# Moving the weight sums of the first up block and of the second gate/up block behind the first gate group's products

## The chip, the cores and the metric

The kernel runs on one core of one Trainium2 chip. The metric is the device time of one execution in microseconds (us); less is better. All times below are of this kernel on such a core. In the profile PE is the matmul engine (TensorE), PEld its weight loads, DVE the vector engine, ACT the scalar engine, POOL GpSimd, and SP the engine that issues most of the DMAs.

## The reference

```python
x  = A_x                                   # 2048 tokens x 1024
xn = layernorm(x)
q, k, v = split_heads(xn @ wqkv)           # 32 heads of 32
o  = phi(q) (phi(k)^T v) / (phi(q) . sum phi(k))
s  = o @ wo                                # the attention branch
g  = silu(xn @ w_gate)                     # 1024 x 3584
u  = xn @ w_up                             # 1024 x 3584
y  = (g * u) @ w_down                      # 3584 x 1024
out = x + s * silu(y)
```

All inputs are bf16. `phi(t)` is `t + 1` for positive `t` and `exp(t)` otherwise, plus 1e-6.

## The kernel before

The work has three stages, and PE goes through them in one order that is written out by hand. The first normalises and transposes the tokens and makes q, k, v and the sums over the tokens; the second makes the attention output and its projection with `wo` (`s_sb`, stored to `s_dram`); the third is the gated network: gate and up products, `h = silu(gate) * up` stored to `h_dram`, and from about 570 us the product with `w_down`.

**Seven products for eight.** Most matrix products are done by blocks of 2 x 2 with seven block products instead of eight, on sums of blocks. In the gate/up stage one *group* is one block of 256 columns of `w_gate` or `w_up` (index `m`, 14 of them; `gu` is 0 for gate and 1 for up) against 1024 tokens (`p`, 2 of them). Each of the seven products (M3, M4, M1, M5, M2, N7, N6) is a set of four matmuls of 128 x 128 by 512, recorded on line 131. M3 and M4 use the weights as loaded (`wg_sb`, `wu_sb`). The other five use sums of weight blocks, which four DVE operations (lines 152 to 155, `wsum_ops`) write to `ws_all`; `sum_w(m, gu)` (line 166) issues these four. `ws_all` has two slots for `m`, used in turn, and two for `gu`.

**A group's steps** (class `Group`, line 994):
- `part_a`: M3 into the accumulator X, then ACT copies X to `n` (line 1007); M4 into Y, then DVE makes `q = n + Y` (line 1011).
- `part_b`: M1 into Z, then DVE makes `u = Z + q` (line 1017); M5 is added onto X, and X goes to the sink on ACT; M2 is added onto Y, and Y goes to the sink on ACT.
- `part_c`: N7 onto X and N6 onto Y, each followed by a DVE subtraction from `u` (line 1026), into `cg` for gate and `up` for up.

X, Y and Z are banks of the accumulator memory, eight in all, taken in turn. The order on PE is: part_a of a group, part_c of the group before it, part_b of the group. So a group's first four sets (its own M3 and M4, the older group's N7 and N6) need no weight sums of its own; M1 is the first that does.

**What sets the order.** In the second stage the order on PE, DVE, ACT, POOL and SP is that of the source (`FRONT_ORDER` and SP, line 921). In the third stage only PE's and POOL's is (`PE_ORDER`, line 987); DVE, ACT and SP get theirs from a scheduler that places an operation once its inputs are there by its own reckoning. Operations of the third stage can be placed by it between those of the second. Each engine then works through its own list in order.

**Around the change.** The end of the second stage projects the last tokens in two groups of the same seven products, `sg` and `sh`, each ending in two DVE subtractions to `s_sb` (line 908), each stored by a DMA that ACT issues (line 884). Between them stand the first two calls of `sum_w`:

```python
            sg.part_c()
            sum_w(0, 0)
            sh.part_b()
            sh.part_c()
            sum_w(0, 1)
```

In the loop of the third stage (line 1186) `sum_w(m + 1, gu)` is issued behind each group's `part_b` when `p` is 0 (line 1220).

`gate(insts, after)` (line 80) adds, for each instruction given, an edge from `after`; with its default it is marked as one without synchronisation, for the scheduler only. `marks["mm"]` is the matmul issued last by `products` (line 131).

Of the kernel before, what the change touches and what calls it, by code (L numbers as in the profile page):

```python
# [21 lines left out]
def kernel(  # L22
# [57 lines left out]
    def gate(insts, after, sync=False):  # L80
        if after is None:
            return
        for d in insts:
            tc.add_manual_dep(d.ins, after.ins.name, SYNCD if sync else SCHED, reason="prefetch gate")

    marks = {}
# [61 lines left out]
    def wsum_ops(w, ws):  # L148

        ws = ws.rearrange("p (k c) -> p k c", k=HD)  # L150
        tt = nc.vector.tensor_tensor
        return [lambda: tt(out=ws[:, :, 0:P], in0=w[:, 0:HD, 0:P], in1=w[:, HD:DC, P:2 * P], op=ALU.add),
                lambda: tt(out=ws[:, :, P:3 * P], in0=w[:, 0:HD, :], in1=w[:, HD:DC, :], op=ALU.add),
                lambda: tt(out=ws[:, :, 3 * P:4 * P], in0=w[:, HD:DC, P:2 * P], in1=w[:, HD:DC, 0:P], op=ALU.subtract),
                lambda: tt(out=ws[:, :, 4 * P:5 * P], in0=w[:, 0:HD, 0:P], in1=w[:, 0:HD, P:2 * P], op=ALU.subtract)]
# [7 lines left out]
    wraw = {}  # L163
    wsum = {}

    def sum_w(m, gu):
        wsum[(m, gu)] = ws_all[:, m % 2, gu]
        for op in wsum_ops(wraw[(m, gu)], wsum[(m, gu)]):
            op()

    def w_operands(m, gu):
        return block_operands(wraw[(m, gu)], wsum[(m, gu)])

    def load_w(m, after=None, sync=False):
        cols = slice(m * FW, (m + 1) * FW)
        wg_sb = wgu.tile([P, DC, FW], BF16, name="wg_sb", tag="wg_sb")
        d1 = nc.sync.dma_start(out=wg_sb[:], in_=wg_v[:, :, cols])
        wu_sb = wgu.tile([P, DC, FW], BF16, name="wu_sb", tag="wu_sb")
        d2 = nc.sync.dma_start(out=wu_sb[:], in_=wu_v[:, :, cols])
        gate([d1, d2], after, sync=sync)  # L180
        wraw[(m, 0)] = wg_sb
        wraw[(m, 1)] = wu_sb
# [573 lines left out]
    with ExitStack() as p2:  # L756
# [12 lines left out]
        def emit_KVZ():  # L769
            for j in range(NJ):  # L770
                g0 = j * GPT
                ng = min(GPT, G - g0)
                nc.vector.tensor_tensor(out=KVZ[:, g0:g0 + ng, 0:P], in0=kvz_ps[j][:, 0:ng, 0:P],
                                        in1=mask[:, None, :].to_broadcast([P, ng, P]), op=ALU.mult)
                nc.vector.tensor_tensor(out=KVZ[:, g0:g0 + ng, P:P + HPG],
                                        in0=kvz_ps[j][:, 0:ng, P:P + 1].to_broadcast([P, ng, HPG]),
                                        in1=sel[:, None, :].to_broadcast([P, ng, HPG]), op=ALU.mult)
# [33 lines left out]
        def emit_OT():  # L811
            while o_ready:
                b, t, o_sb = o_ready.popleft()
                r0 = b * TB + t * P
                nc.scalar.dma_start(out=o_dram[r0:r0 + P, :], in_=o_sb[:])
                nc.sync.dma_start_transpose(out=oT_of(b)[:, :, t * P:(t + 1) * P], in_=o_dram[r0:r0 + P, :])
                if (b, t) in load_at:
                    for m in load_at[(b, t)]:
                        load_w(m)
# [94 lines left out]
        def s_unit():  # L914
            emit_S(*units.popleft())

        def nd_tile():
            if nds:
                emit_ND(*nds.popleft())

        with tc.manual_schedule(engines=FRONT_ORDER | {ET.SP}):

            qb, qc = QGroup(NPASS - 1, NM_Q - 2), QGroup(NPASS - 1, NM_Q - 1)
            for c in range(NCC):
                nc.sync.dma_start(out=wo_sb[:, :, c * CW:(c + 1) * CW], in_=wo_v[:, :, c * CW:(c + 1) * CW])
            emit_KVZ()
            qa.part_b()
            nd_tile()
            qb.part_a()
            emit_OT()  # L930
            qa.part_c()
            nd_tile()
            qb.part_b()
            emit_OT()
            nd_tile()
            qb.part_c()
            emit_OT()


            rows = deque((grp, i) for grp in (qa, qb, qc) for i in range(2))  # L940
            nd_at = {1, 2, 4, 6, 8, 10, 11, 13, 15, 16, 17, 19, 20}
            row_at = {0, 1, 3, 5, 7, 9}
            wo_at = {10, 11, 12, 14, 18}
            sum_at = {23: lambda: groups[0].sums()}
            q_at = {0: qc.part_a, 2: qc.part_b, 3: qc.part_c}
            assert len(nd_at) == len(nds) and len(row_at) == len(rows)
            n7 = TPB * NCC
            groups = [SGroup(t) for t in range(0, TPB, 2)]
            for u in range(len(units) - n7):
                if u in q_at:  # L950
                    q_at[u]()
                if u in nd_at:
                    nd_tile()
                if u in row_at:
                    grp, i = rows.popleft()
                    grp.part_d(i)
                if u in wo_at:
                    out, a, b, op = wo_sums.popleft()
                    gate([nc.gpsimd.tensor_tensor(out=out, in0=a, in1=b, op=op)], marks["phi"], sync=True)
                if u in sum_at:  # L960
                    sum_at[u]()
                s_unit()
                emit_OT()
            sg, sh = groups
            sg.part_a()
            sh.sums()
            sg.part_b()
            sh.part_a()
            sg.part_c()
            sum_w(0, 0)  # L970
            sh.part_b()
            sh.part_c()
            sum_w(0, 1)
    p12.close()
    ps12.close()

# [109 lines left out]
    def slots_x(t):  # L1086
        return t[:].rearrange("p c (h t) -> p (c h) t", t=CW).bitcast(BF16)
# [4 lines left out]
    def slots_w(t):  # L1092
        return t[:].rearrange("p (a b) f -> p a (b f)", f=FW, b=CW // FW)

    def slots_wd(t):
        return t[:].rearrange("p k (a f) -> p (k a) f", f=CW)
# [87 lines left out]
    with tc.manual_schedule(engines=PE_ORDER):  # L1184
        prev = None
        for m, p in order:
            if p == 0 and m + PREF < NM:
                load_w(m + PREF)
            if (m, p) == (NM - 2, 0):
                sl5 = Slots()  # L1190
                for _ in range(2):
                    sl5.add(slots_w(wgu.tile([P, DC, FW], BF16, name="wg_sb", tag="wg_sb")), 4)
                    sl5.add(slots_w(wgu.tile([P, DC, FW], BF16, name="wu_sb", tag="wu_sb")), 4)
                sl1 = Slots()
                for _ in range(2):
                    sl1.add(slots_wd(wdst.tile([P, 2, D], BF16, name="wdr", tag="wdr")), 4)
                for _ in range(2):
                    sl1.add(wdst.tile([P, 3, CW], BF16, name="wdsA", tag="wdsA")[:], 3)
                    sl1.add(wdst.tile([P, 2, CW], BF16, name="wdsB", tag="wdsB")[:], 2)
                WD["M5"] = load_wd("M5", sl5.take(NM))  # L1200
            gs = GateSink()
            for gu in range(2):
                sink = gs if gu == 0 else UpSink(gs, m, p)
                grp = Group(w_operands(m, gu), x_operands(p), HD, sink)
                grp.part_a()
                if prev is not None:
                    prev.part_c()
                if gu == 0 and (m, p) == (NM - 2, NPASS - 1):
                    slx, sls = Slots().add(slots_x(xnT[0]), 16), Slots().add(slots_xs(XS[0]), 20)
                    load_h(0, (NM - 2,))  # L1210
                    WD["M3"] = load_wd("M3", slx.take(NM))
                    WD["M4"] = load_wd("M4", sls.take(NM))
                    sa5 = sls.take(4)
                    spare = Slots()
                    spare.free = sl1.free + sls.free + slx.free + sl5.free
                    WD["M1"] = load_wd("M1", spare.take(NM))
                grp.part_b()
                prev = grp
                if p == 0 and m + 1 < NM:
                    sum_w(m + 1, gu)  # L1220
                if gu == 0 and (m, p) in wd_at:
                    prep_wd(wd_at[(m, p)])
        hp0 = hps[0]
        h0_ops = {"M4": lambda k: hp0[:, 1, k, P:2 * P], "M3": lambda k: hp0[:, 0, k, 0:P]}
        first = Group(h0_ops, WD, NM, None)
        first.part_a()
        prev.part_c()
# [120 lines left out]
```

## Time and profile before

| | us |
|---|---|
| median of 3 runs | 748.28 |
| lowest and highest of them | 747.86, 748.52 |
| the profiled execution | 747.96 |
| its span, first to last instruction | 746.2 |
| granted share of PE's clock | 0.999 |

The span is what the profile covers; the profiled execution is 1.8 us longer than it. The busy time of each engine stands on the page that the prediction shows. A matmul is listed with a duration, but the next one starts before that has passed, so PE's time is best read from start to start. In the timeline each row has its start and its duration in us, the engine, the line, the operation, the tile written and the tiles read; the number in brackets is the time that the engine stood idle just before, and what ended it. In the waits view each row has who waited for whom, the total in us, how often, and the longest.

### The profile page before, as it was taken

Reading aid. Unit: us, or ns where it says so; the run is one execution under the profiler, and the core shown is the slowest. Engines: PE = TensorE matmul, PEld = TensorE weight load, DVE = VectorE, ACT = ScalarE, POOL = GpSimd, SP = SyncE. Lnnn points to the kernel's source line nnn. Section 1 sums busy time; section 2 is a strip of 40 time slices with the busy share of each in tenths; the row PEclk is TensorE's granted clock in tenths of the full one; section 3 lists DMA queues with packets and bytes.
Section 4 is the critical chain, followed back from the end, with each engine's and each line's share of the span. In section 5 each row is a group of like instructions: output and inputs, shape, how many; then the busy total and the mean of one; then the engine's idle time right before and its main releaser. Section 6 shows DMA issues by size and latency. Waiting matters only on the chain.

```text
span 746.2 us, 9886 instructions
## 1 busy us (share of the span) xinstructions
PE 736.9 (99%) x3661; PEld 347.0 (47%) x3700; DVE 517.4 (69%) x955; ACT 272.3 (36%) x476; POOL 69.9 (9%) x106
## 2 busy tenths in 40 slices
PE   9999999999999999999999999999999999999997
PEld 4544444455544444444444444444444444444454
DVE  6889896688768767787678867776655754445554
ACT  4444574755223343434343333434342111111111
POOL 3210000000730000000000000000000221121220
PEclk9999999999999999999999999999999999999999
DMA  9756000316689553655337643455779745554200
GB/s 313 260 161 170 1 0 1 113 44 156 198 230 278 149 149 101 188 174 158 109 97 204 184 127 105 150 161 156 265 255 344 284 171 183 184 184 170 98 29 29
DMA packets 132464, 118.09 MB, mean 158 GB/s; under 512 B 33728, under 2 KB 112704, under 8 KB 131136
## 3 DMA queue, kind: packets, MB, share of 16 engines
q1 hardware_dynamic: 127520, 108.68, 47.1%
q10 hardware_dynamic: 4896, 8.78, 3.5%
q8 instruction: 29, 0.48, 0.3%
q14 instruction: 19, 0.16, 0.1%
HBM read 70.52 MB, written 39.58 MB: 148 GB/s over the span
## 4 chain that ended last, share of the span: by engine, by line
PE 96%; DMA 2%; DVE 1%; issue 0%; ACT 0%; DVEq 0%; ACTq 0%
PE X L131 29%; PE Y L131 29%; PE Z L131 10%; PE kv_ps L455 9%; PE s_ps L829 5%; PE qX L131 3%; PE qY L131 3%; PE kY L131 2%; PE kX L131 2%; DMA wg_sb<-in_B_w_gate_dram 1%; PE nd_ps L790 1%; PE kvz L484 1%; PE qZ L131 1%; PE kZ L131 1%; DMA xp<-in_A_x_dram 0%
## 5 line engine op out<-in xcount | busy, mean ns | idle before, releaser
L131 PEld LDWEIGHTS <-ws_all 128*128 128x128 bf16 x1424 | 138.1, 98 | 164.0 <-issue 1.9
L1011 DVE TENSOR_TENSOR q<-n,Y 128x512 f32<-128x512 f32 x63 | 43.3, 688 | 104.4 <-PE Y L131 103.2
L131 PEld LDWEIGHTS <-xs 128*128 128x128 bf16 (+1 forms) x736 | 69.6, 98 | 76.5
L1281 POOL TENSOR_TENSOR o_out<-y,xres 128x512 bf16<-128x512 f32 x29 | 35.1, 1210 | 495.1 <-DVE y L1280 495.1
L131 PE MATMUL Y<-xs,ws_all 128*128 128x512 f16 (+3 forms) x308 | 70.3, 360 | 0.0
L131 PE MATMUL X<-xnT,ws_all 128*128 128x512 f16 (+1 forms) x278 | 70.1, 379 | 0.2
L131 PE MATMUL Y<-xnT,ws_all 128*128 128x512 f16 x224 | 57.5, 379 | 0.8 <-DVE q L1011 0.8
L131 PE MATMUL X<-xs,ws_all 128*128 128x512 f16 x224 | 57.5, 379 | 0.0
L131 PE MATMUL Z<-xs,ws_all 128*128 128x512 f16 x224 | 57.5, 379 | 0.0
L1135 ACT ACTIVATE g<-cg 128x512 bf16<-128x512 f32 x56 | 35.3, 630 | 54.4 <-DVE cg L1026 54.4
L1017 DVE TENSOR_TENSOR u<-Z,q 128x512 f32<-128x512 f32 x63 | 43.2, 686 | 15.9 <-PE Z L131 15.9
L1135 ACT ACTIVATE g<-X 128x512 bf16<-128x512 f32 x28 | 16.7, 597 | 99.0 <-PE X L131 99.0
L1007 ACT COPY n<-X 128x512 f32<-128x512 f32 x63 | 36.9, 585 | 30.8 <-PE X L131 27.6
L455 PEld LDWEIGHTS <-xnT 128*128 128x128 f16 x320 | 30.7, 98 | 36.0 <-DVE xnT L427 0.5
L1160 DVE TENSOR_TENSOR ho<-g,up 128x1024 bf16<-128x1024 bf16 x56 | 38.2, 685 | 0.5
L455 PE MATMUL kv_ps<-wk_sb,xnT 128*128 128x512 bf16 x156 | 36.9, 379 | 0.6 <-DVE xnT L427 0.3
L1280 DVE TENSOR_TENSOR y<-y,s_in 128x512 f32<-128x512 f32 x31 | 22.2, 717 | 21.4 <-ACT y L1274 15.8
L455 PE MATMUL kv_ps<-wv_sb,xnT 128*128 128x512 bf16 x155 | 35.9, 379 | 0.2
L131 PEld LDWEIGHTS <-wu_sb 128*128 128x128 bf16 x224 | 21.9, 98 | 26.4
L131 PEld LDWEIGHTS <-wg_sb 128*128 128x128 bf16 x224 | 21.9, 98 | 26.4
L1274 ACT ACTIVATE y<-X 128x512 f32<-128x512 f32 x8 | 4.8, 597 | 69.7 <-PE X L131 61.2
L829 PE MATMUL s_ps<-wo_sb,oT 128*128 128x512 bf16 x123 | 29.0, 379 | 0.2
(208 smaller groups left out, 1146.8 us busy)
## 6 DMA issues: line engine op xcount, KB each, us to landing
h_dram<-ho SPq DMA_DIRECT2D x56, 256.0 KB, 2.5
wg_sb<-in_B_w_gate_dram SPq DMA_DIRECT2D x14, 512.0 KB, 4.0
wu_sb<-in_B_w_up_dram SPq DMA_DIRECT2D x14, 512.0 KB, 4.4
wdr<-in_B_w_down_dram SPq DMA_DIRECT2D x14, 512.0 KB, 4.2
ws_all<-h_dram SPq DMA_DIRECT2D x4, 1792.0 KB, 8.7
wds_dram<-wdsA SPq DMA_DIRECT2D x14, 384.0 KB, 2.7
hp_a<-h_dram SPq DMA_DIRECT2D x3, 1792.0 KB, 9.6
o_dram<-o_sb ACTq DMA_DIRECT2D x16, 256.0 KB, 3.1
```

The lines of the kernel that those rows point to most:

```text
L131: marks["mm"] = nc.tensor.matmul(acc[:, 0:c1 - c0], lhsT=lhs(k), rhs=rhs(k)[:, c0:c1], start=(first and k == 0), stop=(k == n - 1), skip_g ...
L455: mm = nc.tensor.matmul(kv_ps[:], lhsT=xn_tok_ap(i)[:, dc, :], rhs=wkv_ap(c)[:, dc, :], start=(dc == 0), stop=(dc == DC - 1))
L484: nc.tensor.matmul(kvz_ps[j][:, gi, 0:P + 1], lhsT=pk_sb[:, g * P:(g + 1) * P], rhs=v_sb[:, g, 0:P + 1], start=(i == 0 and gi == 0), stop= ...
L790: mm = nc.tensor.matmul(nd_ps[:, gi, :], lhsT=pqT_tiles[(p, g // 2)][:, g % 2, t0:t0 + P], rhs=KVZ[:, g, :], start=True, stop=True)
L829: mm = nc.tensor.matmul(s_ps[:], lhsT=oT[:, c, ttok], rhs=wo_sb[:, c, cc * CW:(cc + 1) * CW], start=(c == 0), stop=(c == G - 1))
L1007: nc.scalar.copy(out=n[:], in_=self.X[:])
L1011: nc.vector.tensor_tensor(out=self.q[:], in0=n[:], in1=self.Y[:], op=ALU.add)
L1017: nc.vector.tensor_tensor(out=self.u[:], in0=Z[:], in1=self.q[:], op=ALU.add)
L1135: nc.scalar.activation(out=self.g[:, i, j * TB:(j + 1) * TB], in_=src, func=ACT.Silu)
L1160: nc.vector.tensor_tensor(out=self.ho[:, i], in0=self.g[:, i], in1=self.up[:, i], op=ALU.mult)
L1280: nc.vector.tensor_tensor(out=t[:], in0=t[:], in1=self.s_in[:, i, cs], op=ALU.mult)
L1281: (nc.vector if last and (i, j) != (0, 0) else nc.gpsimd).tensor_tensor(out=self.o_out[:, i, cs], in0=t[:], in1=self.xres[:, i, cs], op=AL ...
```

## The change

`sum_w` returns its four instructions. The call `sum_w(0, 1)` leaves the end of the second stage and goes into the loop of the third, behind `part_b` of the first gate group (`m` 0, `p` 0, `gu` 0), with an edge from the last matmul of that `part_b` (M2). The sums of block 1, issued in the loop at `m` 0, get such an edge too: the gate sums from M2 of the first gate group, the up sums from M2 of the first up group. The calls for all later blocks are as before, with no edge.

```diff
     def sum_w(m, gu):
         wsum[(m, gu)] = ws_all[:, m % 2, gu]
-        for op in wsum_ops(wraw[(m, gu)], wsum[(m, gu)]):
-            op()
+        return [op() for op in wsum_ops(wraw[(m, gu)], wsum[(m, gu)])]
...
             sh.part_b()
             sh.part_c()
-            sum_w(0, 1)
...
                 prev = grp
+                if (m, p, gu) == (0, 0, 0):
+                    gate(sum_w(0, 1), marks["mm"])
                 if p == 0 and m + 1 < NM:
-                    sum_w(m + 1, gu)
+                    sums = sum_w(m + 1, gu)
+                    if m == 0:
+                        gate(sums, marks["mm"])
                 if gu == 0 and (m, p) in wd_at:
```

## The prediction

> **What bounds the kernel now.** I read the shares of busy time first, then what the matmul engine (PE) waited for, then the timeline of the stretch in which the longest of these waits lies. The page and the waits view of PE:
>
> ```profile
> PE 736.9 (99%) x3661; PEld 347.0 (47%) x3700; DVE 517.4 (69%) x955; ACT 272.3 (36%) x476; POOL 69.9 (9%) x106
> ...
> PE w_ps L493 <- DVE warm L90: 1.2, 1, 1.2
> PE Y L131 <- DVE q L1011: 0.8, 1, 0.8
> ```
>
> PE is the bound nearly everywhere: what makes the kernel shorter is time in which PE does not start the next matmul. One listed wait lies inside the work, for the vector engine's (DVE's) `q`. It is at 236.8 us, where the output projection hands over to the first gate/up group. The timeline of PE there (start, duration, four matmuls to a line):
>
> ```profile
> 232.07 1.03 PE L131 MATMUL X<-xs,wg_sb 128*128 128x512 f16 x4
> 232.93 1.03 PE L131 MATMUL Y<-xs,wg_sb 128*128 128x512 f16 x4
> 233.91 1.02 PE L131 MATMUL Z<-xs,ws_all 128*128 128x512 f16 x4
> 234.94 1.02 PE L131 MATMUL X<-xnT,ws_all 128*128 128x512 f16 x4
> 236.79 1.02 PE L131 MATMUL Y<-xnT,ws_all 128*128 128x512 f16 x4 [0.83 <-DVE q L1011]
> 237.65 1.03 PE L131 MATMUL X<-xs,wu_sb 128*128 128x512 f16 x4
> ```
>
> These are M3, M4, M1, M5, M2 of group (m 0, p 0, gate), then M3 of the up group. Count from start to start. An undisturbed set of four takes 0.863 (236.79 to 237.65, and so on). From M4 at 232.93 the next starts should be 233.80, 234.66 and 235.52; they are 233.91, 234.94 and 236.79. So M1 loses 0.11, M5 a further 0.17, M2 a further 0.99: **1.27 us** altogether. Behind it nothing more is lost: M2 starts at 236.79, the first matmul on `hp_a` at 570.03, and between them lie 386 sets (392 of the stage, less the four ahead of M2 and the two of the last part_c, which come later): 333.24 / 386 = 0.863 each.
>
> Here a rule decides how to read the rows. The idle column would give a gain of 0.83, the starts give 1.27. The Trainium skill, Perfetto Trace Analysis, section "Tensor Engine Instruction (MATMUL, LD_WEIGHTS)", says that the end of a matmul in the profile is estimated from its size, not observed. The rows agree: a matmul is listed with 379 ns while the next starts 216 ns after it, so 163 ns of each stall are hidden under the listed duration, and stalls of 0.11 and 0.17 nearly vanish from the idle column.
>
> Who is late? DVE in the same stretch (the number in brackets is its own idle time):
>
> ```profile
> 231.30 0.42 DVE L152 TENSOR_TENSOR ws_all<-wg_sb 128x512 bf16<-128x512 bf16 x1 [0.53 <-DMA wg_sb<-in_B_w_gate_dram]
> 231.64 0.68 DVE L153 TENSOR_TENSOR ws_all<-wg_sb 128x1024 bf16<-128x1024 bf16 x1
> 232.24 0.68 DVE L908 TENSOR_TENSOR s_sb<-qu,sX 128x512 bf16<-128x512 f32 x1
> 232.84 0.42 DVE L154 TENSOR_TENSOR ws_all<-wg_sb 128x512 bf16<-128x512 bf16 x1
> 233.18 0.68 DVE L908 TENSOR_TENSOR s_sb<-qu,sY 128x512 bf16<-128x512 f32 x1
> 233.77 0.42 DVE L152 TENSOR_TENSOR ws_all<-wu_sb 128x512 bf16<-128x512 bf16 x1
> 234.11 0.68 DVE L153 TENSOR_TENSOR ws_all<-wu_sb 128x1024 bf16<-128x1024 bf16 x1
> 234.71 0.42 DVE L154 TENSOR_TENSOR ws_all<-wu_sb 128x512 bf16<-128x512 bf16 x1
> 235.05 0.42 DVE L155 TENSOR_TENSOR ws_all<-wu_sb 128x512 bf16<-128x512 bf16 x1
> 235.38 0.42 DVE L155 TENSOR_TENSOR ws_all<-wg_sb 128x512 bf16<-128x512 bf16 x1
> 235.72 0.42 DVE L152 TENSOR_TENSOR ws_all<-wu_sb 128x512 bf16<-128x512 bf16 x1
> 236.05 0.68 DVE L1011 TENSOR_TENSOR q<-n,Y 128x512 f32<-128x512 f32 x1
> ```
>
> and the scalar engine (ACT):
>
> ```profile
> 233.00 1.26 ACTq L884 DMA_DIRECT2D s_dram<-s_sb  x2
> 234.30 0.58 ACT L1007 COPY n<-X 128x512 f32<-128x512 f32 x1 [3.25 <-PE Y L131]
> ```
>
> The `wg_sb` sums at 231.30 to 232.84 and 235.38 are those of block 1, which the scheduler has put among the last steps of the projection, ahead of both `s_sb` subtractions; the four on `wu_sb` from 233.77 are sum_w(0, 1), then one of block 1's up sums. Three delays follow. M1 starts 0.05 after the second `s_sb` ends (233.86), as it would if Z takes the bank that this subtraction frees. ACT issues the store of this `s_sb` before `n`, so `n` runs from 234.30 to 234.88, and M5, which adds onto X, starts 0.06 later. `q` had its inputs at 234.88 but stands behind the sums until 236.05; it ends at 236.73 and M2, which adds onto Y, starts 0.06 later.
>
> **The change, part by part.** It removes nothing and adds no operation and no DMA: twelve DVE additions move (four for (0, 1), eight for block 1). They pass no queue but DVE's; SP's, POOL's and ACT's instructions stay in number and kind. Four sums occupy 0.34 + 0.60 + 0.34 + 0.34 = 1.62 from start to start (233.77 to 235.38), with 0.08 more until the last has ended.
>
> Ahead of `q`: nothing of the sums may now be scheduled before M2, which itself follows `q`. The first `s_sb` then waits only for PE: its input set, N7 on sX, starts at 230.34 and ends 1.02 later, 231.36. So 231.40 to 232.08 instead of 232.24 to 232.92. The second waits for N6 (231.20 + 1.03 = 232.23): 232.27 to 232.95, 0.91 earlier than now. Both are before 233.80, so M1's 0.11 goes. The store follows and `n` moves by the same 0.91, to 233.39 to 233.97, before 234.66: M5's 0.17 goes. `q` then waits for M4 (232.93 + 1.03 = 233.96) and `n`: 234.03 to 234.71, 0.8 before M2's 235.52: the 0.99 goes. Next late would be `n`: the second store of the group before took 0.97 to issue instead of 0.33 here; with that, `n` ends at 234.6 and `q` at 235.3, still in time.
>
> Behind M2: `u` runs to about 235.5 (M1 ends 234.83). Then come sum_w(0, 1) and the gate sums of block 1. Their cover is the first half of the up group, which uses raw weights: M3 at 236.39, M4 237.25, then N7 238.11 and N6 238.97 of the gate group; M1 of the up group, the first that reads a sum of (0, 1), starts at 239.84.
>
> What the new edge costs no row shows, so two ends. If it only orders, the eight sums run from 235.5 to 238.8, those of (0, 1) done at 237.2. If it makes DVE wait for M2's end (235.52 + 1.02 = 236.54), they run to 239.8, those of (0, 1) done at 238.3. Both are before 239.84. Behind the sums in DVE's queue stands the up group's `q` (ready at 238.3), which M2 of that group needs at 241.56: it ends at 239.5 or 240.5. Behind it the two `cg`, which would end by 241.8 at the latest; their banks are taken again by part_b of the third group, after 245. I take the first end; both cost nothing. Were that cover gone, the four would cost up to 1.70.
>
> The sums of block 1 are read first at 259.23 (Z of group (1, 0, gate)), some 16 us after they are done. Of DVE work, 1.62 + 1.62 + 0.34 = 3.58 moves behind M2; DVE's idle times from 239.6 to 252 add to 1.04 + 0.17 + 0.18 + 2.83 + 1.10 = 5.32, which holds it.
>
> **Sum.** 1.27 gained, 0 added. The profiled execution took 747.96 (span 746.2 and 1.8 around it): 747.96 - 1.27 = 746.69. The median of the runs shown is 0.32 above that execution, so I forecast a median of 748.28 - 1.27 = **747.0**, 0.17% faster. About 0.2% (1.50 us: below 746.78, above 749.78) is what a measurement of this kernel can tell from no change; the gain lies just inside it.
>
> **The rivals.**
> 1. Part of the stall stays: block 1's sums, or other DVE work, still come ahead of `s_sb`. For it: the scheduler interleaved them there once. Against: the edge names a matmul that follows `s_sb` on every path. Then M1 and M5 stay late, M5 at 234.94, M2 at 235.80 when `q` stands directly behind `n`: gain 236.79 - 235.80 = 0.99, so 747.3. If another operation also takes the place ahead of `q`, down to nothing: 748.3.
> 2. The change does not do what it says: the edge is weak and the order on DVE stays as it is: 748.3.
> 3. Slower: the sums of (0, 1) come too late for M1 of the up group. It decides from the point where the last of them ends after 239.84. Worst: DVE takes `q`, both `cg` (the second from 240.04, next start 240.64) and block 1's four sums (1.62, to 242.26) first. M1 then starts at 242.7 if it needs the first sum alone, at 244.0 if all four: 2.9 to 4.2 lost, less 1.27: 749.9 to 751.2. For it: the order is the scheduler's, no longer written by hand. Against: the rows show it placing sums as early as their inputs allow, those written first in front (233.77 before 235.38), and 1.73 lie between M2's end and M4's, time for all four.
>
> **How the numbers follow.** Forecast 0.85, rival 1 0.08, rival 2 0.03, rival 3 0.04. The three runs spread by 0.66, so the forecast's own measured range is 746.5 to 747.5, and about a quarter of it lies below 746.78. Rivals 1 and 2 are within 0.2%. Faster 0.20, same 0.75, slower 0.05. The range takes in rivals 1 and 2 and the spread below: 746.4 to 748.4; rival 3 stays out.
>
> **What would show it.** Right: PE starts 0.86 apart from M3 of the first gate group through the up group's M2, no wait of Y for `q`, `s_sb` directly behind the projection's sets, `n` near 233.4, the sums behind `u`. Wrong: a `ws_all` row between the `s_sb` rows, a PE wait for `ws_all` in the up group, or a new gap further on, where now there is none.

## The result, and the profile after

| | before | changed |
|---|---|---|
| median of 17 runs each, taken side by side, us | 748.16 | 746.73 |
| lowest and highest | 747.37, 749.44 | 746.30, 747.74 |
| ratio, with its 95% interval | | 0.9982 (0.9974 to 0.9989) |
| profiled execution, us | 747.96 | 747.54 |
| its span, us | 746.18 | 745.75 |

The changed kernel is 0.18% faster; the interval stands for 0.8 to 1.9 us. The two profiled executions differ by only 0.42, and that has to be explained too. The page and the waits view of PE, for the changed kernel (lines behind the moved call have numbers lower by one or two):

```profile
PE 737.4 (99%) x3661; PEld 347.7 (47%) x3700; DVE 517.6 (69%) x955; ACT 272.1 (36%) x476; POOL 71.2 (10%) x106
...
PE w_ps L492 <- DVE warm L90: 1.2, 1, 1.2
PE kv_ps L454 <- DVE xnT L426: 0.3, 1, 0.3
```

The shares are the same to a per cent, so they tell nothing; the wait of Y for `q` is gone. The timeline of PE in the stretch of the change, from M3 of the first gate group through M2 of the up group:

```profile
232.91 1.03 PE L131 MATMUL X<-xs,wg_sb 128*128 128x512 f16 x4
233.77 1.03 PE L131 MATMUL Y<-xs,wg_sb 128*128 128x512 f16 x4
234.64 1.03 PE L131 MATMUL Z<-xs,ws_all 128*128 128x512 f16 x4
235.50 1.03 PE L131 MATMUL X<-xnT,ws_all 128*128 128x512 f16 x4
236.36 1.03 PE L131 MATMUL Y<-xnT,ws_all 128*128 128x512 f16 x4
237.23 1.03 PE L131 MATMUL X<-xs,wu_sb 128*128 128x512 f16 x4
...
240.68 1.03 PE L131 MATMUL Z<-xs,ws_all 128*128 128x512 f16 x4
```

Every step is 0.86. All three stalls have gone, and none has come at Z of the up group (240.68). DVE and ACT in the same stretch:

```profile
232.25 0.69 DVE L907 TENSOR_TENSOR s_sb<-qu,sX 128x512 bf16<-128x512 f32 x1 [0.62 <-PE sX L131]
233.11 0.69 DVE L907 TENSOR_TENSOR s_sb<-qu,sY 128x512 bf16<-128x512 f32 x1 [0.17 <-PE sY L131]
234.89 0.69 DVE L1009 TENSOR_TENSOR q<-n,Y 128x512 f32<-128x512 f32 x1 [1.09 <-ACT n L1005]
235.76 0.69 DVE L1015 TENSOR_TENSOR u<-Z,q 128x512 f32<-128x512 f32 x1 [0.17 <-PE Z L131]
236.36 0.41 DVE L152 TENSOR_TENSOR ws_all<-wu_sb 128x512 bf16<-128x512 bf16 x1
...
239.24 0.42 DVE L155 TENSOR_TENSOR ws_all<-wg_sb 128x512 bf16<-128x512 bf16 x1
239.58 0.68 DVE L1009 TENSOR_TENSOR q<-n,Y 128x512 f32<-128x512 f32 x1
```

```profile
234.24 0.58 ACT L1005 COPY n<-X 128x512 f32<-128x512 f32 x1 [2.33 <-PE X L131]
```

No `ws_all` row stands between the two `s_sb` any more, DVE now waits for PE and ACT ahead of `q`, and the eight sums follow `u`.

**How the spans add up.** Two marks on PE cut the span into parts: the start of M4 of the first gate group (before 232.93, after 233.77) and the first matmul on `hp_a` (before 570.03, after 569.61). Between them lie the three stalls and, by the starts, nothing else that differs (from M2 to the second mark it is 333.24 before and 333.25 after): 337.10 before and 335.84 after, a gain of **1.27 us**, to the rounding. From the second mark to the end it is 176.15 and 176.14. But the first projection matmul (`kv_ps`) starts at 7.22 in one profile and at 8.24 in the other: 1.02 lost at the very front, in code that the change does not touch. From there to M4 it is 225.71 and 225.54. Together -1.27 + 1.02 - 0.17 - 0.01 = -0.43, the difference of the spans. So the profiled pair hides most of the gain, and the stretch from M4 to `hp_a` is the measure used below, beside the ratio of times. What it has over the 335.84 of the changed kernel is called the stall.

### The profile page after: what moved, and what is told of

It reads as the page before. It is cut to its first block, busy times and chain, and to the rows that moved or that the text cites. A ratio compares the mean times of both kernels' runs of the same rounds, so it can differ in the third digit from the quotient of the medians.

```text
span 745.8 us, 9884 instructions
## 1 busy us (share of the span) xinstructions
PE 737.4 (99%) x3661; PEld 347.7 (47%) x3700; DVE 517.6 (69%) x955; ACT 272.1 (36%) x476; POOL 71.2 (10%) x106
## 4 chain that ended last, share of the span: by engine, by line
PE 98%; DVE 1%; issue 0%; ACT 0%; DVEq 0%
PE X L131 29%; PE Y L131 29%; PE Z L131 10%; PE kv_ps L454 9%; PE s_ps L828 5%; PE qX L131 3%; PE qY L131 3%; PE kY L131 2%; PE kX L131 2%; PE nd_ps L789 1%; PE kvz L483 1%; PE qZ L131 1%; PE w_ps L492 1%; PE sX L131 1%; PE kZ L131 1%; PE sY L131 1%
```

## The experiments

The theories. **A**: the sums of block 1, put ahead of the two `s_sb`, are the cause; M1 and M5 hang on `s_sb`, M2 on `q`, each by itself. Its rival **B**: each sum ahead of `q` has its share, so the move of (0, 1) carries most of the gain. **C** says that M1 of the up group needs all four sums, **F** that only what is ahead of `s_sb` counts. **D** and its rival **E** came out of the first four runs.

| kernel | ratio to before (95%) | M4 to `hp_a`, us | stall in it |
|---|---|---|---|
| before | | 337.10 | 1.27 |
| changed | 0.9982 (0.9974 to 0.9989) | 335.84 | 0.00 |
| only block 1 held | 0.9985 (0.9977 to 0.9994) | 335.84 | 0.00 |
| only (0, 1) moved | 0.9993 (0.9984 to 1.0002) | 337.52 | 1.68 |
| block 1 held to the projection's end | 0.9990 (0.9982 to 0.9999) | 336.20 | 0.36 |
| sums of (0, 1) mid up group | 1.0000 (0.9992 to 1.0009) | 336.60 | 0.76 |
| all eight sums late | 1.0027 (1.0016 to 1.0038) | 338.47 | 2.63 |
| true wait | 0.9986 (0.9976 to 0.9995) | 335.84 | 0.00 |
| before, late load | 1.0063 (1.0049 to 1.0078) | 340.31 | 4.47 |
| changed, late load | 0.9982 (0.9973 to 0.9991) | 335.84 | 0.00 |
| before, early load | 0.9993 (0.9984 to 1.0003) | 336.56 | 0.72 |
| before, second profile | one execution, 747.72 us | 336.56 | 0.72 |
| before, third profile | one execution, 748.14 us | 337.55 | 1.71 |

**Which half of the change does it? Only block 1 held:**

```diff
             sh.part_c()
+            sum_w(0, 1)
...
-                if (m, p, gu) == (0, 0, 0):
-                    gate(sum_w(0, 1), marks["mm"])
```

(The diffs of this section are against the changed kernel unless the text says otherwise.)

> Only the edges on block 1's sums; sum_w(0, 1) stays at the end of the projection. Theory A (block 1's sums, put ahead of s_sb, are the whole cause; the four sums of (0, 1) alone still leave q in time): in the clock of the kernel before, s_sb at 231.4 and 232.3, the four sums from 232.9, q from 234.5 to 235.2, M2 at 235.52 undisturbed: the full 1.27 us, ratio 0.9983, and from M4 of the first gate group to the first matmul on hp_a 335.8 us. Rival B (each of the six sums ahead of q has its share, so the move of the four of (0, 1) carries most of the 0.99): 0.28 for M1 and M5 and about a third of 0.99, some 0.6 us, ratio 0.9992, 336.5 us.

Measured: 335.84, the whole gain. DVE of that kernel:

```profile
233.05 0.69 DVE L907 TENSOR_TENSOR s_sb<-qu,sY 128x512 bf16<-128x512 f32 x1 [0.18 <-PE sY L131]
233.65 0.42 DVE L152 TENSOR_TENSOR ws_all<-wu_sb 128x512 bf16<-128x512 bf16 x1
...
235.26 0.68 DVE L1010 TENSOR_TENSOR q<-n,Y 128x512 f32<-128x512 f32 x1
236.07 0.69 DVE L1016 TENSOR_TENSOR u<-Z,q 128x512 f32<-128x512 f32 x1
```

The four sums of (0, 1) still stand ahead of `q`, which ends at 235.94; M2 starts undisturbed at 236.30. Rival B falls: four sums ahead of `q` cost nothing, as `q` still ends 0.36 before M2 starts. The move of (0, 1) makes that margin larger (0.78 in the changed kernel); it saves no time.

**Only (0, 1) moved:**

```diff
-                    if m == 0:
-                        gate(sums, marks["mm"])
```

> Only sum_w(0, 1) is moved, with its edge; block 1's sums are left free. Theory A: they stay ahead of s_sb and the freed places ahead of q are taken by block 1's other sums, five of them instead of six: M1 0.11 and M5 0.17 late as before, q 0.33 earlier, so a gain of 0.33 us, ratio 0.9996, 336.8 us from M4 of the first gate group to the first matmul on hp_a. Rival B: q is freed of four of the six sums, 1.4 us, so M2 follows M5 and the gain is about 0.99, ratio 0.9987, 336.1 us.

Measured: 337.52, worse than either theory said, and in this profile 0.41 more than before. The timeline shows why:

```profile
232.13 0.43 DVE L152 TENSOR_TENSOR ws_all<-wg_sb 128x512 bf16<-128x512 bf16 x1 [1.36 <-DMA wg_sb<-in_B_w_gate_dram]
...
236.56 0.68 DVE L1009 TENSOR_TENSOR q<-n,Y 128x512 f32<-128x512 f32 x1
```

```profile
234.74 1.02 PE L131 MATMUL Z<-xs,ws_all 128*128 128x512 f16 x4 [0.70 <-DVE s_sb L907]
235.77 1.02 PE L131 MATMUL X<-xnT,ws_all 128*128 128x512 f16 x4
237.28 1.02 PE L131 MATMUL Y<-xnT,ws_all 128*128 128x512 f16 x4 [0.49 <-DVE q L1009]
```

DVE waited 1.36 for block 1's gate weights, where it had waited 0.53 in the first profile of before. From M4 (233.01) to that first sum it is -0.88 here against -1.63 there (231.30 less 232.93): 0.75 later, of which the one sum fewer ahead of `q` gives 0.33 back: 1.27 + 0.75 - 0.33 = 1.69, and 1.68 is measured. So theory A's 0.33 is there, and something that it left out is larger: DVE stands behind a load that does not land equally far ahead of M4 in each execution. The row of Z also names `s_sb`, as the prediction had supposed for M1. The times of this kernel alone would not decide: the profiled execution was the slowest of its eleven (748.46, median 747.22), and the interval of the ratio, 0.9984 to 1.0002, holds both A's 0.9996 and B's 0.9987. What decides against B is the kernel above, with only block 1 held.

**D: the loss of the kernel before hangs on that load.** Three runs move the landing, two repeat the kernel before. The late load, made on the kernel before and on the changed one, is this edit:

```diff
-                        load_w(m)
+                        wraw[(m, 0)] = wgu.tile([P, DC, FW], BF16, name="wg_sb", tag="wg_sb")
+                        wraw[(m, 1)] = wgu.tile([P, DC, FW], BF16, name="wu_sb", tag="wu_sb")
+                    for m in (0, 2, 1):
+                        cols = slice(m * FW, (m + 1) * FW)
+                        nc.sync.dma_start(out=wraw[(m, 0)][:], in_=wg_v[:, :, cols])
+                        nc.sync.dma_start(out=wraw[(m, 1)][:], in_=wu_v[:, :, cols])
```

> The kernel before, with the loads of block 1 issued behind those of block 2; the order on DVE is that of before. Theory D (block 1's sums ahead of s_sb also make DVE wait for their load, so the loss of the kernel before hangs on when that load lands): wg of block 1 lands near 235.8 instead of 231.2, DVE stands until then, s_sb ends near 238.4, q near 241.3, M2 starts some 5.8 late instead of 1.27: ratio about 1.006, 341.6 us from M4 of the first gate group to the first matmul on hp_a. Theory E (only the time of the sums themselves counts, the load is there in time): as before, 337.1 us, ratio 1.000.

> The changed kernel with the same exchange of the loads. Theory D: DVE reaches block 1's sums behind u and the four sums of (0, 1), near 237.1 in the clock of the kernel before, when the load has landed (235.8): no difference from the changed kernel, 335.8 us from M4 to hp_a, ratio 0.998. If block 1's loads were still on the path: up to 4 us slower.

The changed kernel does not notice it: 335.84 and a ratio of 0.9982. The kernel before is 0.63% slower; M4 to `hp_a` is 340.31, not 341.6, since the load landed earlier in this profile than I had assumed (DVE starts on it at 233.50, not near 235.8). The profiled execution, 750.92, was also the fastest of the four; the other three took 753.04 to 753.59. They have no trace, so what made them slower still, a later landing or a lower clock for longer, is not shown. DVE and PE in the profiled one:

```profile
233.50 0.43 DVE L152 TENSOR_TENSOR ws_all<-wg_sb 128x512 bf16<-128x512 bf16 x1 [2.90 <-DMA wg_sb<-in_B_w_gate_dram]
```

```profile
232.68 1.03 PE L131 MATMUL Y<-xs,wg_sb 128*128 128x512 f16 x4
236.11 1.02 PE L131 MATMUL Z<-xs,ws_all 128*128 128x512 f16 x4 [2.40 <-DVE s_sb L913]
237.14 1.86 PE L131 MATMUL X<-xnT,ws_all 128*128 128x512 f16 x4
238.99 1.79 PE L131 MATMUL Y<-xnT,ws_all 128*128 128x512 f16 x4
240.61 1.03 PE L131 MATMUL X<-xs,wu_sb 128*128 128x512 f16 x4
```

The early load is made on the kernel before by the same edit with another order of issue, `(0, 0), (1, 0), (0, 1), (1, 1), (2, 0), (2, 1)` for (m, gu).

> The kernel before, with the load of block 1's gate weights issued second, ahead of the up weights of block 0; the order on DVE is that of before. Theory D: the load has landed when DVE comes to the sums (230.7 in the clock of the kernel before), the second of them waits for N7 of the projection (231.4) instead, all behind it is 0.22 earlier: M1 undisturbed, M2 1.05 late instead of 1.27: 336.9 us from M4 of the first gate group to the first matmul on hp_a, ratio 0.9997. Rival (the load is the whole stall): no loss, 335.8 us, ratio 0.998.

> The kernel before, unchanged, for one more profile. Theory D: its loss between M4 and hp_a is 1.27 plus the time by which wg of block 1 lands later than 1.72 ahead of M4 (where it lands earlier, not under 1.05), to 0.1 us; beyond about 2.5 us of stall the lower clock adds to it. Theory E: 1.27 in each profile, whatever the landing.

> As b1: the kernel before, unchanged, for one more profile. Theory D: a loss of 1.27 plus the lateness of the landing against 1.72 ahead of M4, to 0.1 us. Theory E: 1.27.

The first sum of block 1 (its first row of L152) in the third profile of before, and in the second, where DVE comes to it without a listed wait:

```profile
231.47 0.42 DVE L152 TENSOR_TENSOR ws_all<-wg_sb 128x512 bf16<-128x512 bf16 x1 [0.90 <-DMA wg_sb<-in_B_w_gate_dram]
```

```profile
230.47 0.68 DVE L899 TENSOR_TENSOR qu<-qu,sZ 128x512 f32<-128x512 f32 x1
231.06 0.42 DVE L152 TENSOR_TENSOR ws_all<-wg_sb 128x512 bf16<-128x512 bf16 x1
```

One number carries all of them: the start of this row against the start of M4.

| profile of the kernel before | L152 less M4, us | stall by 1.27 + (that + 1.63) | measured |
|---|---|---|---|
| second (M4 at 233.23) | -2.17 | 0.73 | 0.72 |
| early load (230.48, M4 at 232.65) | -2.17 | 0.73 | 0.72 |
| first | -1.63 | 1.27 | 1.27 |
| third (M4 at 232.66) | -1.19 | 1.71 | 1.71 |
| late load (M4 at 232.68) | +0.82 | 3.72 | 4.47 |

Theory E, 1.27 each time, falls. The chain view of the first profile (228 to 240 us) begins with that load, issued at 221.72 and landed 9.49 later:

```profile
221.72 9.49 DMA wg_sb<-in_B_w_gate_dram
```

In the three profiles of the kernel before the load took 8.6 (second), 9.5 (first) and 9.8 us (third) and landed at 230.8, 231.2 and 231.4, while M4 started at 233.23, 232.93 and 232.66. So the load moved by 0.6 and M4 by 0.57 the other way: about half of the spread is that PE itself came later, which gave the load more time. Where the load is there in time, 0.72 is left: that much is DVE's work alone, by the sums of block 1 among `s_sb` and ahead of `q`. My floor of 1.05 was wrong: I had let the second sum wait for the end of N7 on sX, and in the early-load profile it starts at 230.82, right behind the first. In the late load the formula holds to M2's start (238.99, where 232.68 + 3 x 0.863 = 235.27 would be undisturbed: 3.72); the other 0.75 is a lower clock, below.

**Does M2 hang on `q` by itself? Block 1 held to the projection's end**, with sum_w(0, 1) there too:

```diff
             sh.part_c()
+            proj_end = marks["mm"]
+            sum_w(0, 1)
...
-                if (m, p, gu) == (0, 0, 0):
-                    gate(sum_w(0, 1), marks["mm"])
...
-                        gate(sums, marks["mm"])
+                        gate(sums, proj_end)
```

> Block 1's sums are held until the last matmul of the projection, no longer; sum_w(0, 1) stays at the end of the projection. One sum of block 1 then comes between the two s_sb, one more (0.60) ahead of q. Theory A (M1 and M5 hang on s_sb, M2 on q, each by itself): M1 and M5 undisturbed, q from 235.2 to 235.9 in the clock of the kernel before, M2 0.4 late: gain 0.9, 336.2 us from M4 to hp_a, ratio 0.9988. Rival F (what counts is only what stands ahead of s_sb): the full gain, 335.8 us, ratio 0.9983.

```profile
233.60 1.03 PE L131 MATMUL Z<-xs,ws_all 128*128 128x512 f16 x4
234.47 1.03 PE L131 MATMUL X<-xnT,ws_all 128*128 128x512 f16 x4
235.69 1.02 PE L131 MATMUL Y<-xnT,ws_all 128*128 128x512 f16 x4 [0.20 <-DVE q L1011]
```

```profile
234.36 0.68 DVE L153 TENSOR_TENSOR ws_all<-wg_sb 128x1024 bf16<-128x1024 bf16 x1
234.96 0.68 DVE L1011 TENSOR_TENSOR q<-n,Y 128x512 f32<-128x512 f32 x1
```

Measured 336.20, as A said. M1 (233.60) and M5 are on time, M2 alone is 0.36 late. F falls: one sum of 0.60 too many ahead of `q` is enough, even with `s_sb` cured. (Block 1's other sum, 0.34 long, lies between the two `s_sb`, most of it in a gap that was there.)

**The other side: sums too late.** First sum_w(0, 1) alone, held from M2 to the middle of the up group:

```diff
+                if (m, gu) == (0, 1):
+                    wsum[(0, 1)] = ws_all[:, 0, 1]
...
                     prev.part_c()
+                if (m, p, gu) == (0, 0, 1):
+                    gate(sum_w(0, 1), marks["mm"])
...
-                if (m, p, gu) == (0, 0, 0):
-                    gate(sum_w(0, 1), marks["mm"])
```

> As the changed kernel, but sum_w(0, 1) is held until the last matmul of the gate group's part_c, in the middle of the up group. Theory A (q and s_sb are cured as in the changed kernel; M1 of the up group waits for the first of the four sums alone, M5 for the second): the first sum comes between the two cg and ends at 240.2 in the clock of the kernel before, so M1 some 0.6 late, the second ends at 241.4, so M5 some 1.0 late in all: of 1.27 gained 0.3 is left, 336.8 us from M4 of the first gate group to the first matmul on hp_a, ratio 0.9996. Rival C (M1 waits until the last of the four sums has ended, 242.1): 2.5 late, 1.2 slower than before, 338.3 us, ratio 1.0016.

```profile
240.23 0.42 DVE L152 TENSOR_TENSOR ws_all<-wu_sb 128x512 bf16<-128x512 bf16 x1
...
241.16 0.68 DVE L153 TENSOR_TENSOR ws_all<-wu_sb 128x1024 bf16<-128x1024 bf16 x1
```

```profile
240.70 1.04 PE L131 MATMUL Z<-xs,ws_all 128*128 128x512 f16 x4 [0.25 <-DVE ws_all L152]
241.90 1.04 PE L131 MATMUL X<-xnT,ws_all 128*128 128x512 f16 x4 [0.16 <-ACT g L1133]
```

M1 starts 0.05 after the first sum has ended (240.65), M5 0.06 after the second (241.84). The view names ACT's `g` for M5, but the weights of M5, which are read from `ws_all`, are loaded at 241.89, 0.05 after the second sum has ended, and M5 follows at once; the last to come was L153. So A holds (each product waits for its own sum), C falls, and the loss is 0.76 where I expected 1.0: I had added 0.2 for the load of the weights into the array, and that took no such time.

Then the slower rival of the prediction, brought about: block 1's gate sums first, then those of (0, 1), both held there.

```diff
                 if (m, p, gu) == (0, 0, 1):
+                    gate(sum_w(1, 0), marks["mm"])
                     gate(sum_w(0, 1), marks["mm"])
...
-                if p == 0 and m + 1 < NM:
+                if p == 0 and m + 1 < NM and (m, gu) != (0, 0):
```

(against the kernel just above)

> As the changed kernel, but the four gate sums of block 1 and then the four of (0, 1) are held until the last matmul of the gate group's part_c: the slower rival of the prediction, made on purpose. Theory A (M1 needs the first sum of (0, 1) alone): that sum ends at 242.4 in the clock of the kernel before, M1 starts near 242.7 instead of 239.84, 2.8 to 2.9 lost, less 1.27: 1.6 us slower than before, ratio 1.0021, 338.7 us from M4 of the first gate group to the first matmul on hp_a. Rival C (all four needed): 4.2 lost, 2.9 slower, ratio 1.0039, 340.0 us. If the loss is taken up further on, no change against the changed kernel: 335.8 us.

```profile
239.05 1.03 PE L131 MATMUL Y<-xs,ws_all 128*128 128x512 f16 x4
242.54 1.04 PE L131 MATMUL Z<-xs,ws_all 128*128 128x512 f16 x4 [2.46 <-DVE ws_all L152]
```

2.63 lost, nothing of it taken up later, and 1.0027 (1.0016 to 1.0038) in time. The cover under the moved sums is real, and it ends where the prediction put it.

**A true wait** on the edges (`sync=True` in both new calls of `gate`):

> The changed kernel with the edges made real: DVE waits for M2 of the first gate group ahead of sum_w(0, 1), and for M2 of the first up group ahead of block 1's up sums. Theory A (2.6 us of slack before M1 of the up group): the first sum 0.3 to 0.5 later than in the changed kernel, nothing on PE: 335.8 us from M4 to hp_a, ratio 0.998. Rival: the wait delays q of the up group past its M2: some tenths of a microsecond more, 336.0 to 336.5 us.

```profile
236.49 0.43 DVE L152 TENSOR_TENSOR ws_all<-wu_sb 128x512 bf16<-128x512 bf16 x1 [0.91 <-PE Y L131]
...
239.71 0.68 DVE L1009 TENSOR_TENSOR q<-n,Y 128x512 f32<-128x512 f32 x1
```

DVE really waits (0.91 for PE), and PE loses nothing: 335.84. Both ends of the unknown cost were free, as bounded.

## Why the prediction was right, and where it was short

- **Reading the stalls from start to start**: right. 0.11, 0.17 and 0.99 have all gone, 1.27 together, where the idle column had shown 0.83. The forecast median was 747.0, the measured one 746.73, inside the range.
- **What can be told from no change**: the prediction put that at about 0.2%. With 17 executions each the interval of the ratio ends at 0.9989, so a gain of 0.18% could be told.
- **The rows behind them**: right to 0.02. In the clock of before (0.84 less, by the two starts of M4), the first `s_sb` starts at 231.41 (forecast 231.40), `n` at 233.40 (233.39), `q` at 234.05 (234.03), the eight sums run from 235.52 to 238.82 (235.5 to 238.8).
- **The cover behind M2, and the edge**: right. The slack to M1 of the up group, the wait that costs nothing, and the price of the cover gone were each run by itself. For the slower rival I gave 2.9 to 4.2; 2.63 is measured, since M1 needs the first sum alone and the sums before it fitted closer.
- **The parts**: I gave the two halves one sum. The edges on block 1 do it all; the move of (0, 1) is worth nothing beside them, as DVE's time ahead of `q` had room for four sums.
- **The step that was short**: "The profiled execution took 747.96 ... 747.96 - 1.27 = 746.69." I took the stall of one execution for that of all. The row at 231.30 said otherwise, with 0.53 of waiting for a DMA: the stall has a fixed 0.72 and a part that follows the landing against M4, 0 to 0.99 in three profiles of the same kernel. That the forecast came so near is in part luck: the one profile that it rests on lay in the middle of the three. The measured gain, 1.43 between the medians, fits a stall that moves between 0.72 and 1.71 as well as one of 1.27 each time; the interval (0.8 to 1.9 us) cannot tell these apart.
- **The forecast for the profiled execution** (746.69) missed by 0.85: it came out at 747.54, by the slow front, 1.02, less the 0.17 between front and M4. The spread of the runs was in the range, its cause was not in the text.

What stays open: how the landing is spread over many executions, and so the mean of the stall in the kernel before. Three profiles are too few for it.

## What to carry to other kernels

An operation that is early by the scheduler's reckoning is not free on an engine that works in order: look at what stands behind it, and above all at a wait for a DMA there, because it ties the whole queue to a landing that moves from run to run (here by a microsecond against the work that waits for it). Hold such work behind the last operation that the bound engine needs, and count the cover up to its own first reader. And compare two profiles between marks that only the change can move: here the front alone moved by 1.02, against a gain of 1.27.

## What the runs showed of the hardware

**The granted clock fell after a stall of 2.6 us, once.** In the kernel before with the late load, PE stood from 233.5 to 236.1. The table by stretches of that kernel (stretch, its length, PE's busy time and matmuls, granted clock, DMA share, GB/s):

```profile
232.60:236.10 3.50, 1.11 (x6) 1.00 1.17 316
236.10:237.50 1.40, 1.38 (x5) 0.87 1.15 285
237.50:239.00 1.50, 1.50 (x5) 0.50 1.14 359
239.00:240.60 1.60, 1.60 (x5) 0.51 0.28 104
240.60:242.00 1.40, 1.40 (x8) 1.00 0.00 1
```

From 237.1 to 240.6 matmuls start about 0.43 us apart instead of 0.216; of this 0.75 us is lost beyond the stall. In the kernel with all eight sums late PE stood as long (2.62), and the clock stayed at 1.00. So the "about 2.5 us" in the expectation of the second profile is no limit that these runs bear out. The Trainium skill, TensorE: Matmul & The Clock Gate, section "What's actually happening", has a free-running window of some 3.4 us, an idle one of which halves the clock. The halving and the 3.5 us for which it lasted agree. But a stall of 2.6 us cannot fill such a window, and the clock fell all the same; here the measurement decides. Whether such a stall is enough may be a matter of how it lies to the window, which no run here shows.

**The front of the kernel moves by a microsecond.** The kernel begins with 14 matmuls that only warm PE up. Before and after, they take:

```profile
1.19 4.89 PE L493 MATMUL w_ps<-warm 128*128 128x512 bf16 x14 [1.19 <-DVE warm L90]
```

```profile
1.19 6.15 PE L492 MATMUL w_ps<-warm 128*128 128x512 bf16 x14 [1.19 <-DVE warm L90]
```

They start 0.43 apart at first and 0.22 apart later. I read the step as a rise of the clock, since 0.43 is the spacing that goes with a granted clock of 0.50 in the table above; the granted clock itself is listed as 1.00 in this stretch of both profiles, so it does not show the rise. In the first profile of before the step was at about 4.7 us, in its second at 6.3, in the profile of the changed kernel not before 7.1; the first `kv_ps` then starts at 7.22, 7.75 and 8.24. Over all thirteen profiles it lies between 7.10 and 8.24. This, and not the change, is what made the two profiled executions differ by 0.42 only.
